# A chunked RWKV-6 recurrence and a star-ReLU layer in one kernel: turning tiles on TensorE instead of the DMA crossbar, and totals of log w through DRAM

## The chip, the cores and the metric

The kernel runs on one core of a Trainium2 chip. The core has TensorE (PE, the matrix unit, which reads SBUF and writes PSUM), VectorE (DVE), ScalarE (ACT) and GpSimd (POOL, which here works on SBUF only), a queue SP that issues DMAs, and 16 DMA engines that move the data. Each engine works through its own instruction list in order; semaphores tie the lists together. The time is the device time of one launch in microseconds. The kernel's time before is 183.34 us, the median of three runs (183.16 to 183.92).

## The reference

Two layers. The first is a recurrence over 768 steps, for 4 batches and 8 heads of width 48; the second is a feed-forward layer on its 3072 x 384 output.

```python
# attention: r, k, v, w are (4, 8, 768, 48), u is (8, 48)
state = zeros((B, H, D, D))
for t in range(S):
    cur = einsum('bhd,bhe->bhde', u[None] * k[t], v[t])
    y[t] = einsum('bhd,bhde->bhe', r[t], state + cur)
    state = w[t][..., None] * state + einsum('bhd,bhe->bhde', k[t], v[t])
# feed-forward: x = y as (3072, 384); w_in (384, 2048); w_out (2048, 384)
h = x @ w_in
g = s * relu(h) ** 2 + b
out = g @ w_out
```

All inputs and the output are float32 in DRAM. w lies between 0.8 and 0.95.

## The kernel before

The sequence is cut into chunks of 128 steps, so there are 6 chunks x 4 batches = 24 chunk-batches, numbered n = 0 to 23 in the order of work. The first four are handled in pairs with a packed layout; from 4 on each goes by itself, chunk by chunk over the four batches, so that n + 4 is the next chunk of the same batch. Two chunk-batches make one token tile T of 256 tokens, 12 tiles in all.

One chunk-batch takes these steps; the words are those of the order (below), the lines those of the kernel before.

- `load n.x` (L297): w, r, k, v by SP, 192 KB each. `ln` (L329, ACT): log w into a bf16 tile whose heads are padded from 48 to 64 columns.
- `cum` (L383, PE): exclusive running sums of log w over the chunk, by a product with a triangular matrix, into PSUM (`cums`). For chunks that are not the last of the sequence, four more products with one column of ones (L416) give the chunk's total of log w per channel, with channels on partitions: columns 384 to 387 of the same PSUM tile. Last chunks (n of 20 and above) need no totals.
- `exp` (L424, ACT): exp of the running sums, and of the totals in the same instruction (388 columns). From n = 6 on, `inc` (L460, DVE) adds log w to the running sum to make it inclusive, and `exn` (L471, ACT) takes exp of its negative.
- `mul` (L477, DVE): r and k times these, into `prd` (bf16, 128 x 1024 with padding).
- `tr` (L533, PE) turns `prd` with eight products against the identity into a PSUM tile `trps`, and `tev` (L556) copies that to the SBUF tile `RK`. For n >= DTK = 9 there is no `tr`; `tev` is then one DMA transpose on SP (`dtrans`, L572), from SBUF to SBUF.
- `mt` (L589, PE): k-by-r products per head, for a pair of chunk-batches. `msk` (L625, DVE) masks them. `ymm` (L640, PE): the chunk's output, from the masked products and from the state that came in. `yev` (L751, DVE) adds the diagonal term `yd`, which POOL and DVE make by `rkp`, `rku`, `cd`, `yd` (L343 to L381).
- `dmm` (L713, PE), `sup` (L765, DVE) and `st` (L791, POOL) make the new state: new = (old + d) * exp(total), where `l2` (L510, POOL) spreads exp of the totals over two column groups. The state is needed by `ymm` and `sup` of n + 4.
- `xtr` (L800, PE) turns the output x (three products) and `xev` (L814) copies it into `xT`, the token tile's operand. For n >= DTX = 18 one DMA transpose (`dxtr`, L581) does both.

Per token tile follow 8 blocks `g1` (L851, PE, six products of 256 columns: x by w_in), each followed by `relu` (L869, ACT) and `sq` (L877, ACT or DVE), and 8 blocks `g2` (L894, PE, four products of 384 columns: g by w_out), `oev` (L909, DVE) and `store` (L922, SP). The feed-forward weights are loaded in five pieces (`li`, `lo`) and cast to bf16 (`ci`, `co`) early on.

The order of all this is written out by hand in a text, ORDER (L41): every word is one step, and the engines get their instructions in that order. `@A`, `@D`, `@P` after a word put the step on ACT, DVE or POOL; `+9` stands for nine warm-up products on PE. A table of rings (L970) holds how many buffers each kind of tile has: `P=6` PSUM buffers serve `cum`, `tr`, `mt`, `xtr`, `ymm`, `dmm` and `g1` alike, `rh=4` buffers stand between relu and square. The planner only verifies that the text respects the dependencies and the rings; its costs set nothing on the chip.

There is also code for taking totals by DMA (`lam`, `lamg`, `by_row`); with LAM = 24 no chunk-batch uses it before the change.

Of the kernel before, what the change touches and what calls it, by code (L numbers as in the profile page):

```python
# [8 lines left out]
FP32 = mybir.dt.float32  # L9
# [16 lines left out]
PKD = 1.55  # L26
ONE = 6
DTK = 9
DTX = 18
DK2 = 24  # L30
DX2 = 24
LAM = 24
# [9 lines left out]
load0.0 load0.2 +9 load0.1 ln0 load2.2 cum0.0 load0.3 cum1.0 exp0.0 +1 u_mm exp0.1 load2.0 exp1.0  # L42
rkp0 mul0.0 load2.1 cum1.1 mul0.1 exp1.1 rkp1 load4.0 u_ev@D tr0 mul1.0 +4 tev0@A mul1.1 rku1 li0
tr1 load2.3 exl0 +2 rku0 cd1 tev1@A li1 ln2 cd0 mt0 load4.1 msk1.0 cum2.0 rkp3 l21 li2 msk0.0 +2 yd1
ln4 exp2.0 cum3.0 cum3.1 msk0.1 l20 rku3 ci0@A load4.2 msk1.1 cum4.0 +3 vb0@D vb1@A yd0 mul2.0
exp2.1 lo0 dmm0 exp3.1 mul2.1 +2 li3 exp3.0 li4 exl2 mul3.0 exp4.0 l23 cum4.1 sup0 vb3@P ymm0.0
exp4.1 tr2 rkp2 ci1@A mul3.1 st0 ymm0.1 sup1 ydm0 vb2@A l24 lo1 rku2 ymi0 yev0@D tr3 yev1@A tev2@D
xtr0 tev3@A xtr1 l22 +1 st1 xev0@D cd2 xev1@A mt2 cd3 rkp4 ci2@A g10.0 msk3.0 yd3 g10.1 msk2.0
relu0.0 lo2 msk2.1 yd2 ymm2.0 relu0.1 g10.2 msk3.1 rku4 dmm2 mul4 relu0.2 ymm2.1 ydm2 co0@A ci3@P
g10.3 sq0.1@A sup2 yev2@A cd4 st2 ymi2 sq0.2@A xtr2 sup3 yev3@A csred0@D lo3 g10.4 sq0.0@A ci4@D  # L50
load5.0 xev2@A xtr3 g10.5 load6.0 relu0.3 co1@D xev3@A lo4 g10.6 csred1@D sq0.3@A load5.1 g11.0
relu0.6 csadd1@D g11.1 relu0.4 co2@D relu0.5 g20.0 csred2@D sq0.4@A g10.7 sq0.6@A g11.2 sq0.5@A
relu0.7 g11.3 csadd2@D relu1.0 load5.2 g20.1 co3@D relu1.3 g20.4 relu1.1 load6.1 csred3@D ln5 g20.5
ln6 tr4 sq0.7@A cum6.0 csadd3@P tev4@D cum5.0 relu1.2 g11.4 inc6 sq1.3@A load6.2 g11.5 sq1.0@A co4@D
cum5.1 exp5.0 g11.6 small2 csred4@D exp5.1 load5.3 exp6.0 g20.6 exn6 g11.7 relu1.6 mul5 relu1.4
small g20.7 sq1.1@A load4.3 csadd4@D g20.2 relu1.7 load7.0 cssplit tr5 sq1.2@A load8.0 relu1.5 mul6
csspread g20.3 csevac load8.1 tev5@D vb5@P tr6 sq1.5@A rkp5 oev0.0 tev6@A mt4 load9.0 oev0.1 g21.4
l25 msk4.0 sq1.4@A rku5 load7.1 dmm5 g21.0 vb4@A msk5.0 g21.5 ln7 load7.2 sup5 rkp6 sq1.7@A msk4.1
cum7.0 st5 yd4 dmm4 load8.2 g21.1 load9.1 ln8 exp7.0 sup4 l26 cum8.0 cd5 st4 ymm4 ln9 msk5.1 yd5
g21.6 sq1.6@A inc7 load6.3 ymm5 exp8.0 st3 yev4 cum9.0 exn7 g21.7 yev5 rku6 inc8 xtr4 xtr5 g21.2  # L60
xev4@A load10.0 mul7 l27 xev5@A g21.3 exn8 load9.2 inc9 rkp7 g12.0 oev1.1 exp9.0 load9.3 g12.1 mul8
relu2.0 l28 relu2.1 load7.3 g12.2 cd6 l29 sq2.1@A sq2.0@D yd6 g12.3 load11.0 tr7 load10.1 exn9
oev1.0 relu2.2 g12.4 tev7@D vb6@P relu2.3 load8.3 g12.5 relu2.4 sq2.3@D mul9 sq2.4@A mt6 relu2.5
g22.4 msk7.0 store0.0 sq2.2@A vb7@P g12.6 msk6.0 sq2.5@A rkp9 load11.1 tev9 msk6.1 dmm6 g22.0
relu2.6 rku7 ln10 sup6 g12.7 load10.2 ln11 msk7.1 tr8 rku9 relu2.7 cd7 g22.1 sq2.7@A cum10.0 cd9
tev8@A load12.1 vb9@A dmm7 ymm6 rkp8 inc10 g22.5 rku8 yev6 load12.0 cum11.0 sup7 g22.6 yd9 xtr6
inc11 exp11.0 exp10.0 g22.2 yd7 xev6@A cd8 load15.0 ymm7 sq2.6@A vb8@P mt8 yev7 exn11 load13.0 st6
g22.3 exn10 msk8.0 st7 store0.1 xtr7 g22.7 xev7@D load11.2 msk8.1 rkp10 dmm9 load10.3 g13.0 store1.1
msk9.0 l210 g13.1 rku10 msk9.1 relu3.0 load11.3 g13.2 sq3.0@A sup9 yd8 mul10 g13.3 relu3.2 load12.2
st9 g13.4 ln12 relu3.1 g13.5 oev2.0 sq3.1@A ymm9 oev2.1 relu3.3 dmm8 g13.6 mul11 rkp11 relu3.4 rku11  # L70
sq3.3@A g13.7 load14.0 load13.1 sq3.2@A g23.0 sup8 relu3.5 g23.4 yev9 relu3.6 sq3.4@D l211 tev11
load13.2 sq3.5@A ymm8 cum12.0 relu3.7 yev8 xtr9 vb11@P g23.1 st8 ln13 inc12 tev10 xtr8 sq3.7@D g23.5
xev8@A exp12.0 g23.6 xev9@D store1.0 exn12 vb10@D load12.3 sq3.6@D cum13.0 ln14 dmm11 mul12 g14.0
exp13.0 ln15 g14.1 inc13 tev12 cd10 g23.2 exn13 cd11 load14.1 relu4.1 yd10 dmm10 g14.2 sup10 rkp13
g23.3 sup11 relu4.2 load14.2 mul13 g14.3 sq4.1@A rkp12 relu4.0 g14.4 oev3.0 relu4.3 tev13 mt10
sq4.0@A rku13 g23.7 relu4.4 load15.1 msk10.0 sq4.3@A g14.5 msk10.1 l213 sq4.2@A l212 rku12 msk11.0
cum14.0 g14.6 relu4.5 msk11.1 load13.3 exp14.0 st10 cum15.0 exp15.0 g14.7 oev3.1 vb12@A ymm11 inc15
load17.0 relu4.7 yd11 ymm10 sq4.4@D sq4.5@A g24.4 store2.0 st11 relu4.6 sq4.7@A g24.0 cd12 load16.0
inc14 load15.2 exn14 sq4.6@A rkp14 g24.5 yd12 cd13 mt12 yev10 load16.1 vb13@A rku14 yev11 g24.1
msk12.0 g24.6 msk12.1 store2.1 xtr10 xtr11 load19.1 msk13.0 g24.2 xev10@A xev11@A msk13.1 dmm12 ln16  # L80
g24.7 exn15 cd14 load16.2 g15.0 rkp15 mul14 g15.1 relu5.0 l215 g15.2 relu5.1 load19.2 sup12 g15.3
sq5.0@A mul15 dmm13 st12 relu5.2 ymm12 g24.3 relu5.3 load14.3 sup13 sq5.3@A oev4.1 g15.4 rku15
sq5.2@A yev12 g15.5 ln17 tev15 sq5.1@D yd13 tev14 relu5.4 ymm13 g15.6 oev4.0 cd15 load15.3 st13
cum17.0 relu5.6 xtr12 g15.7 xev12@D relu5.5 rkp16 yev13 g25.4 sq5.4@A load17.1 inc17 sq5.6@A l214
load18.0 g25.0 cum16.0 rku16 relu5.7 inc16 store3.0 xtr13 vb14@A rkp19 g25.5 xev13@D store3.1
exp17.0 exp16.0 g25.1 load17.2 l217 sq5.5@A rku19 load18.1 g16.0 load17.3 dmm14 yd15 g16.1 relu6.0
sup14 exn16 cd16 yd14 relu6.1 mt14 exn17 g25.6 msk14.0 load19.0 vb15@A g16.2 msk14.1 sq5.7@A
load16.3 mul16 g16.3 rkp17 sq6.0@A relu6.2 g16.4 msk15.0 g25.2 msk15.1 sq6.1@A relu6.3 load18.2
rku17 ln18 g16.5 sq6.3@A mul17 g16.6 tev16 st14 sq6.2@A dmm15 relu6.6 load20.3 cum18.0 ymm14 sup15
relu6.4 g25.7 cd19 l216 tev17 relu6.5 g25.3 vb16@P oev5.1 ln19 st15 g16.7 oev5.0 load20.0 rkp18  # L90
ymm15 exp18.0 vb17@D relu6.7 g26.0 yev14 sq6.4@A load21.0 inc18 rku18 cum19.0 xtr14 yev15 exn18
g26.4 inc19 xev14@A l218 g26.5 store4.1 sq6.5@A load22.0 sq6.7@A xtr15 dmm17 g26.1 load20.1 xev15@D
exp19.0 mul18 sq6.6@A g17.0 load18.3 exn19 sup17 dmm16 g17.1 relu7.0 sup16 cd17 g17.2 relu7.1
sq7.0@D g17.3 mul19 relu7.2 yd17 load19.3 g17.4 ln20 st17 relu7.3 mt16 load21.1 sq7.3@A g26.2
msk17.0 relu7.4 load20.2 ln21 st16 g26.3 msk16.0 sq7.2@A g17.5 msk17.1 yd16 store4.0 sq7.1@A
load21.2 msk16.1 cum21.0 g26.6 vb18@P tev19 oev6.0 ln22 l219 g17.6 vb19@P relu7.5 sq7.4@D inc21
store5.1 yd19 ymm17 relu7.6 tev18 ymm16 cum20.0 g27.4 yev16 rkp20 exp20.0 load23.0 yev17 exp21.0
g27.5 exn21 inc20 rku20 xtr16 sq7.5@D xtr17 g26.7 xev16@A load21.3 exn20 rkp21 dmm19 xev17@D g17.7
cd18 g18.0 sup19 relu7.7 rku21 mul20 store5.0 g18.1 sq7.7@A vb20@P yd18 cum22.0 g27.6 relu8.0 g18.2
oev6.1 tev20 exp22.0 mul21 relu8.1 load22.1 g18.3 sq7.6@A supn20 load22.2 relu8.2 g18.4 relu8.3  # L100
g27.0 inc22 sq8.0@A supn21 dmm18 cd20 mt18 sq8.1@D tev21 sup18 g27.7 relu8.4 msk19.0 sq8.3@A
# [1225 lines left out]
```

## Time and profile before

| | |
|---|---|
| median of three runs | 183.34 us |
| the profiled execution | 183.5 us, span 181.7 us |
| PE busy | 171.8 us, 95% |
| DVE / ACT / POOL busy | 142.8 / 142.2 / 105.0 us |
| DMA transposes | 15 of `prd`, 6 of `x_sb` |
| granted TensorE clock | 1.00 |
| DMA moved | 34.72 MB, mean 191 GB/s |

The span goes from the first instruction to the last; the time of the execution has 1.8 us more around it. Busy time is a union: two instructions that overlap on one engine count once. PE's products are pipelined, and the end of each is modelled, so that a product's own duration (273 ns for 256 columns) is longer than its distance to the next. The chain of waits is followed back from the last instruction; it gives each piece of work the time by which it moved the end.

### The profile page before, as it was taken

Reading aid. Unit: us, or ns where it says so; the run is one execution under the profiler, and the core shown is the slowest. Engines: PE = TensorE matmul, PEld = TensorE weight load, DVE = VectorE, ACT = ScalarE, POOL = GpSimd, SP = SyncE. Lnnn points to the kernel's source line nnn. Section 1 sums busy time; section 2 is a strip of 40 time slices with the busy share of each in tenths; the row PEclk is TensorE's granted clock in tenths of the full one; section 3 lists DMA queues with packets and bytes.
Section 4 is the critical chain, followed back from the end, with each engine's and each line's share of the span. In section 5 each row is a group of like instructions: output and inputs, shape, how many; then the busy total and the mean of one; then the engine's idle time right before and its main releaser. Section 6 shows DMA issues by size and latency. Waiting matters only on the chain.

```text
span 181.7 us, 4868 instructions
## 1 busy us (share of the span) xinstructions
PE 171.8 (95%) x1874; PEld 131.9 (73%) x1876; DVE 142.8 (79%) x257; ACT 142.2 (78%) x279; POOL 105.0 (58%) x139
## 2 busy tenths in 40 slices
PE   7989879998999989999999999999999999999993
PEld 2455669765686769688689688787877696888762
DVE  7679999999999979798998497898998976330222
ACT  3589899998889559979878899898896188479920
POOL 3889860229599699559869759289809560000000
PEclk9999999999999999999999999999999999999999
DMA  5999999999898998999989889999994794220013
GB/s 154 323 324 343 387 350 274 260 184 206 167 207 178 187 187 182 199 171 183 232 186 195 212 172 202 208 199 243 160 206 100 158 238 153 69 60 11 0 43 132
DMA packets 116554, 34.72 MB, mean 191 GB/s; under 512 B 110898, under 2 KB 114739, under 8 KB 116531
## 3 DMA queue, kind: packets, MB, share of 16 engines
q1 hardware_dynamic: 116528, 34.42, 81.6%
q8 instruction: 14, 0.23, 0.5%
q14 instruction: 10, 0.07, 0.1%
q10 hardware_dynamic: 2, 0.00, 0.0%
HBM read 25.17 MB, written 4.72 MB: 164 GB/s over the span
## 4 chain that ended last, share of the span: by engine, by line
PE 64%; DVE 10%; DMA 7%; POOL 6%; issue 5%; ACT 4%; SPq 1%; DVEq 0%; ACTq 0%; POOLq 0%
PE o_ps L901 27%; PE h_ps L858 26%; DMA wo_st<-in_moe_w_out_dram 4%; DMA rkt<-in_k_dram 3%; PE mt_ps L617 2%; POOL rkp L346 2%; PE y_ps L676 2%; DVE prd L489 2%; PE y_ps L667 2%; POOL rku L352 1%; POOL yd L375 1%; PE d_ps L741 1%; ACT rh L871 1%; PE cums L410 1%; PE xt_ps L804 1%
## 5 line engine op out<-in xcount | busy, mean ns | idle before, releaser
L901 PE MATMUL o_ps<-w_out,gT 128*128 128x384 bf16 (+2 forms) x400 | 71.8, 320 | 0.5 <-ACT gT L881 0.5
L858 PE MATMUL h_ps<-xT,w_in 128*128 128x256 bf16 x576 | 70.9, 273 | 1.1 <-POOL w_in L983 0.6
L871 ACT ACTIVATE rh<-h_ps 128x512 bf16<-128x512 f32 x96 | 54.4, 597 | 16.6 <-PE h_ps L858 15.7
L858 PEld LDWEIGHTS <-w_in 128*128 128x128 bf16 x576 | 59.9, 110 | 6.1 <-issue 1.0
L901 PEld LDWEIGHTS <-gT 128*128 128x128 bf16 x400 | 36.1, 98 | 19.7 <-ACT gT L881 0.7
L881 ACT ACTIVATE gT<-rh 128x512 bf16<-128x512 bf16 x78 | 47.4, 634 | 0.5
L352 POOL TENSOR_TENSOR rku<-rkp,u_bc 128x384 f32<-128x384 f32 x24 | 27.7, 1158 | 2.2 <-DVE cd L369 1.6
L346 POOL TENSOR_TENSOR rkp<-rkt 128x384 f32<-128x384 f32 x20 | 21.3, 1068 | 11.2 <-DMA rkt<-in_k_dram 9.4
L629 DVE TENSOR_TENSOR mt_sb<-mt_ps,tri_strict 128x512 bf16<-128x512 f32 x40 | 25.4, 681 | 1.9 <-PE mt_ps L617 1.8
L375 POOL TENSOR_TENSOR yd<-vt,cd 128x384 bf16<-128x384 f32 x20 | 17.6, 884 | 11.0 <-DVE cd L369 10.7
L489 DVE TENSOR_TENSOR prd<-rkt,E 128x768 bf16<-128x768 f32 x20 | 23.7, 1187 | 0.3 <-ACT E L473 0.3
L912 DVE SCALAR_TENSOR_TENSOR o_sb<-o_ps,s_bc,bconst 128x384 f32<-128x384 f32 (+2 forms) x25 | 14.6, 594 | 6.4 <-PE o_ps L901 6.3
L883 DVE TENSOR_TENSOR gT<-rh 128x512 bf16<-128x512 bf16 x18 | 9.6, 536 | 10.2 <-ACT rh L871 10.2
L793 POOL TENSOR_TENSOR st<-stmp,l 128x384 bf16<-128x384 bf16 x16 | 15.5, 972 | 0.8 <-DVE stmp L784 0.8
L758 DVE TENSOR_TENSOR x_sb<-y_ps,yd 128x384 bf16<-128x384 f32 x20 | 10.7, 549 | 5.3 <-PE y_ps L676 5.2
L369 DVE TENSOR_REDUCE cd<-rku 128x8 f32<-128x384 f32 x24 | 12.8, 542 | 1.4 <-POOL rku L352 1.4
L448 ACT ACTIVATE E<-cums 128x388 f32<-128x388 f32 (+1 forms) x22 | 10.4, 496 | 4.3 <-DVE inc L463 2.4
L784 DVE TENSOR_TENSOR stmp<-d_ps,st 128x384 bf16<-128x384 f32 x16 | 8.7, 550 | 3.2 <-PE d_ps L741 3.1
L473 ACT ACTIVATE E<-inc 128x384 f32<-128x384 f32 x18 | 9.3, 525 | 1.5 <-DVE inc L463 1.4
L1286 PE MATMUL warm_ps<-warm_sb 128*128 128x512 bf16 x22 | 7.7, 477 | 1.3 <-DVE warm_sb L1242 1.2
L983 POOL CAST vb<-vt 128x384 bf16<-128x384 f32 x9 | 5.6, 629 | 4.1 <-DMA vt<-in_v_dram 4.1
L676 PE MATMUL y_ps<-vb,mt_sb 128*128 128x48 bf16 x160 | 7.3, 183 | 0.0
(112 smaller groups left out, 200.6 us busy)
## 6 DMA issues: line engine op xcount, KB each, us to landing
wt<-in_w_dram SPq DMA_DIRECT2D x20, 192.0 KB, 3.9
rkt<-in_r_dram SPq DMA_DIRECT2D x20, 192.0 KB, 3.8
rkt<-in_k_dram SPq DMA_DIRECT2D x20, 192.0 KB, 3.7
vt<-in_v_dram SPq DMA_DIRECT2D x20, 192.0 KB, 3.6
out_dram<-o_sb SPq DMA_DIRECT2D x19, 192.0 KB, 3.0
wi_st<-in_moe_w_in_dram SPq DMA_DIRECT2D x3, 768.0 KB, 7.5
wo_st<-in_moe_w_out_dram SPq DMA_DIRECT2D x3, 768.0 KB, 7.0
pkt<-in_w_dram SPq DMA_DIRECT2D x2, 384.0 KB, 4.1
```

Of the source, the lines that this page charges most:

```text
L346: nc.gpsimd.tensor_tensor(out=rkp, in0=c["r"], in1=c["k"], op=ALU.mult)
L352: nc.gpsimd.tensor_tensor(out=rku.rearrange("t h d -> t (h d)"), in0=c["rkp"].rearrange("t h d -> t (h d)"), in1=u_bc, op=ALU.mult,)
L369: nc.vector.reduce_sum(out=cd, in_=c["rku"], axis=AX.X)
L375: nc.gpsimd.tensor_tensor(out=yd, in0=c["v"], in1=c["cd"].unsqueeze(2).to_broadcast([128, H, D]), op=ALU.mult,)
L489: nc.vector.tensor_tensor(out=prd[:, :, :, 0:D], in0=c["rk"], in1=c["E"][:, :, 0:HD].rearrange("t x (h d) -> t x h d", h=H), op=ALU.mult,)
L629: nc.vector.tensor_tensor(out=c["mt"][:, sg], in0=c["mt_ps"][sg], in1=(masks[:, n % 2] if packed(n) else tri_strict) .unsqueeze(1) .to_bro ...
L793: nc.gpsimd.tensor_tensor(out=c["st_new"], in0=c["stmp"].rearrange("q p (g e) -> q p g e", g=2), in1=c["l2"].unsqueeze(3).to_broadcast([12 ...
L858: nc.tensor.matmul(ps[:, f, :], lhsT=w_in_sb[PIECE[ft]][:, kt, :].rearrange("p (m j) -> p j m", j=PIECES[PIECE[ft]])[:, ft - F0[PIECE[ft]] ...
L871: nc.scalar.activation(out=rh, in_=hs[T, i], func=AF.Relu)
L881: nc.scalar.activation(out=g, in_=rh, func=AF.Square)
L901: nc.tensor.matmul(os_[T, k][:, cols], lhsT=gT[T][:, ft, tt * 128 : (tt + 1) * 128], rhs=w_out_sb[PIECE[ft]][:, ft - F0[PIECE[ft]], cols], ...
L912: nc.vector.scalar_tensor_tensor(out=o_sb[:, cols], in0=os_.pop((T, k))[:, cols], scalar=s_bc, in1=bconst[:, cols], op0=ALU.mult, op1=ALU.add,
```

## The change

Six things change together.

1. DTK, DTX, DK2, DX2 go to 99: no chunk-batch uses the DMA crossbar. All 24 are turned by `tr` and `tev`, and all 24 outputs by `xtr` and `xev`.
2. LAM goes to 9: chunk-batches 9 to 19 take their totals of log w by DMA. `lam` writes row 127 of the inclusive sums, 512 padded floats, to a DRAM row; `lamg` reads it back so that channels lie on partitions, four floats each; `exl` on ACT takes the exp, and `l2` stays on POOL. The four one-column products of these eleven are gone.
3. The inclusive sums go to two fixed tiles with heads padded to 64 columns (`incs`), the padding cleared once, so that one DMA reads the row back instead of two.
4. `sq` may go to POOL; 16 of 96 do.
5. The warm-up operand shares its memory with `cs_sum`, and the clearing of `lams` goes.
6. ORDER is a new text: 1160 words instead of 1105. The engines of many `tev`, `xev`, `vb`, `co` and `sq` change with it, and the loads' order too.

```diff
-DTK = 9
-DTX = 18
-DK2 = 24
-DX2 = 24
-LAM = 24
+DTK = 99
+DTX = 99
+DK2 = 99
+DX2 = 99
+LAM = 9
...
+    incs = [const.tile([128, H, 64], FP32, name=f"inc{i}", tag=f"inc{i}") for i in range(2)]
...
         if x == 0:
             E = work.tile([128, 2, HD + 16], FP32, name="E", tag="E", bufs=2)
-            c["E"], c["lam"] = E, E[:, 0, HD : HD + HP]
+            c["E"] = E
             if cc < NCH - 1 and not by_row(n):
+                c["lam"] = E[:, 0, HD : HD + HP]
                 w = HD + HP
...
     def expl(n):
         c = cb[n]
+        if not packed(n):
+            t = work.tile([128, 16], FP32, name="lamr", tag="lamr", bufs=NLT)
+            c["lam"] = t[:, 0:HP]
+            nc.scalar.activation(out=c["lam"], in_=lams[:, n % NLT, 0:HP], func=AF.Exp)
+            return
...
     def incl(n):
         c = cb[n]
-        t = work.tile([128, HD], FP32, name="inc", tag="inc", bufs=2)
+        t = incs[incl_no[0] % 2]
+        if incl_no[0] < 2:
+            nc.vector.memset(t[:, :, D:64], 0.0)
+        incl_no[0] += 1
+        c["inc_row"] = t.rearrange("t h d -> t (h d)")[127:128]
+        c["inc"] = t[:, :, 0:D]
...
     def lamrow(n):
         c = cb[n]
-        c["tot"] = dram.tile([1, HD], FP32, name="tot", tag="tot")
-        nc.sync.dma_start(out=c["tot"], in_=c["inc"][127:128])
+        c["tot"] = dram.tile([1, H * 64], FP32, name="tot", tag="tot")
+        nc.sync.dma_start(out=c["tot"], in_=c["inc_row"])
 
     def lamget(n):
-        row = cb[n]["tot"].rearrange("o (p g d) -> g d (o p)", g=2, p=HP)
-        t = lams[:, n % NLT, 0 : 2 * HP].rearrange("q (p g) -> q g p", g=2)
-        for g in range(2):
-            nc.sync.dma_start(out=t[64 * g : 64 * g + D, g], in_=row[g])
+        nc.sync.dma_start(
+            out=lams[:, n % NLT, 0:HP],
+            in_=cb[n]["tot"].rearrange("o (p q) -> q (o p)", q=128),
+        )
...
         if pl.ops["sq", T, i]["eng"] == "ACT":
             nc.scalar.activation(out=g, in_=rh, func=AF.Square)
         else:
-            nc.vector.tensor_tensor(out=g, in0=rh, in1=rh, op=ALU.mult)
+            eng = nc.gpsimd if pl.ops["sq", T, i]["eng"] == "POOL" else nc.vector
+            eng.tensor_tensor(out=g, in0=rh, in1=rh, op=ALU.mult)
...
-    warm_sb = const.tile([128, 2 * TOK], BF16, name="warm_sb", tag="warm_sb")
+    warm_sb = cs_sum.rearrange("p x n -> p (x n)")[:, 0 : 2 * TOK]
...
-    nc.gpsimd.memset(lams, -10000.0)
```

Two stretches of the new text, the second from the end, show how the words stand (`tr` and `tev` of batches 9 and 8, then the squares of the last tile on POOL):

```
tr8 exp10.0 yev7 g22.1 yev6 rku9 relu2.7 sq2.7@A load11.3 vb8@A cum11.0 tr9 tev8@D sq2.6@A st7
load15.0 xtr6 st6 tev9@A xtr7 store0.0 g22.6 exn10 vb9@D exp11.0 xev6@D g22.2 rkp10 inc11 load13.0
xev7@D g22.7 cd8 g13.0 cd9 lamg9 exn11 mul10 relu3.0 g13.1 store0.1 g13.2 mul11 relu3.1 load10.3
...
sq10.7@D g29.2 g210.5 xev23@D sq10.4@A g29.3 g111.0 oev9.0 g111.1 relu11.0 g111.2 sq10.6@P sq11.0@P
store9.0 relu11.1 g111.3 relu11.2 sq11.1@A g210.0 g210.6 sq11.2@D g111.4 g111.5 relu11.4 g111.6
sq11.4@P relu11.5 g210.7 relu11.3 g111.7 oev10.1 sq11.3@D relu11.7 store10.1 g210.1 sq11.7@P g210.2
g210.3 g211.0 oev10.0 g211.1 sq11.5@A relu11.6 sq11.6@P g211.4 g211.2 g211.5 store10.0 g211.3 g211.6
```

## The prediction

> **What bounds the kernel now.** I read the page's busy shares and slices first, then busy time by stretch, then the chain that ended last, then the costliest groups, and the DMA issues last.
>
> ```profile
> PE 171.8 (95%) x1874; PEld 131.9 (73%) x1876; DVE 142.8 (79%) x257; ACT 142.2 (78%) x279; POOL 105.0 (58%) x139
> ...
> PEclk9999999999999999999999999999999999999999
> DMA  5999999999898998999989889999994794220013
> ```
>
> TensorE (PE) is busy 95% of the span at its full granted clock. The 16 DMA engines are nearly as full, which would make them a suspect; the stretches decide. Their columns are length, then busy time and count of PE, of its weight loads, of VectorE (DVE), ScalarE (ACT) and GpSimd (POOL), then clock, DMA share and GB/s.
>
> ```profile
> 1.20:60.00 58.80, 54.01 (x630) 38.39 (x633) 54.21 (x99) 50.41 (x97) 38.90 (x58) 1.00 1.00 262
> 60.00:160.00 100.00, 99.17 (x1096) 78.99 (x1095) 83.44 (x148) 79.82 (x161) 65.54 (x76) 1.00 0.87 182
> 160.00:181.70 21.70, 18.58 (x152) 14.49 (x150) 4.82 (x10) 12.01 (x23) 0.00 (x0) 1.00 0.15 51
> ```
>
> From 60 to 160 us PE stands still for 0.8 us of 100, although DMA is at 0.87. Before 60 it stands still for 4.8 us, with DVE at 54.21 of 58.80. After 160 it stops only for the last store, 3.1 us. The chain (start, length, what) says whether "busy" is really full:
>
> ```profile
> 59.46 0.45 PE trps L538 x8
> ...
> 67.36 3.93 PE h_ps L858 x36
> ...
> 73.14 1.30 PE o_ps L901 x8
> ...
> 75.05 0.19 PE xt_ps L804 x3
> ...
> 75.89 0.17 PE xt_ps L804 x3
> ...
> 77.52 0.08 PE cums L416 x4
> ```
>
> 36 products of 256 columns in 3.93 us are 109 ns each and 8 of 384 columns in 1.30 us are 162 ns each, back to back, block after block: nothing to squeeze. So behind the first 60 us every microsecond of PE work that is added is a microsecond of time, and one removed is one saved.
>
> ```profile
> L881 ACT ACTIVATE gT<-rh 128x512 bf16<-128x512 bf16 x78 | 47.4, 634 | 0.5
> ...
> L793 POOL TENSOR_TENSOR st<-stmp,l 128x384 bf16<-128x384 bf16 x16 | 15.5, 972 | 0.8 <-DVE stmp L784 0.8
> ...
> L554 DVE COPY RK<-trps 128x1024 bf16<-128x1024 bf16 x4 | 2.7, 684 | 0.4 <-PE trps L538 0.2
> ...
> L554 DVE COPY xT<-xt_ps 128x384 bf16<-128x384 bf16 x7 | 2.5, 352 | 2.3 <-PE xt_ps L804 2.3
> ```
>
> These price the evacuations (mean ns behind the comma).
>
> ```profile
> RK<-prd SPq DMA_TRANSPOSE x15, 3.7
> xT<-x_sb SPq DMA_TRANSPOSE x6, 2.6
> ...
> b_bc<-in_moe_b_dram SPq DMA_DIRECT2D x1, 0.5 KB, 3.0
> ```
>
> The 21 crossbar turns land 3.7 and 2.6 us after their issue; the first is issued at 58.0 us, so all lie in the stretch in which PE is full.
>
> **The change, part by part.** *Turns.* 15 chunk-batches (9 to 23) get `trans`: 8 products, 0.45 us by the chain. 15 x 0.45 = +6.75. Six (18 to 23) get `xtr`: 3 products, 0.17 to 0.19, +1.1. All of it lies where PE has no idle time, on the path.
>
> A page of the Trainium skill speaks against this part more than my row does: "TensorE: Matmul & The Clock Gate", section "Back-to-back issue gap", gives about 81 ns for each product of 128 columns in a real stream. The row gives 0.45/8 = 56 ns. By the page the 15 x 8 + 6 x 3 = 138 added products would be an estimated 11.2 us, and the whole sum an estimated 194.4. The same page (Part 4) says that transposes do not count as PE work for the clock; this trace has 126 of them with the clock at 1.00 throughout. The row decides.
>
> *One-column products.* `cum` of batches 9 to 19 loses its four products: 0.08 us by the chain, 11 x 0.08 = -0.9. Warm-up products go from 24 to 23: -0.2, in the head.
>
> PE sum: 6.75 + 1.1 - 0.9 - 0.2 = **+6.7**.
>
> *Evacuations and who pays.* By the two word lists, DVE copies 17 RK tiles instead of 4 (+13 x 0.684 = 8.9), 15 xT instead of 7 (+2.8) and casts three more vb (+1.6), and loses three w_out casts (-2.5): +11 in all. ACT loses 15 squares (-9.5) and gains 11 exps of four columns, RK copies and casts: about -3. POOL gains 16 squares of 128x512 and loses five casts. No row has such a square on POOL: from below a cast of half its operands, 629 ns for 384 columns, so 0.84; from above `rku` in f32, 1158 ns for 384, so 1.54. I take 1.3, scaled from L793 (972), the nearest: bf16 with bf16. POOL comes to about 105 + 16 x 1.3 - 3 = 123 of 190, still the emptiest. These engines are beside the path as long as PE does not wait for them. In 60 to 160, where some 11 us of the DVE work land, DVE goes from 83.4 in 100 to about 95 in 107: 89%. The cover is thin, so I bound what PE waits for. From below 0: in 80 to 100 us before, DVE is at 18.11 of 20 and PE at 20.00. From above 8: in 40 to 60 DVE is at 19.61 of 20 and PE idle 1.51, times 107/20. A second look at the same cost: before, PE waited 1.3 + 0.7 + 0.4 us at the nine batches that it turned itself, 0.27 each, times 15 = 4.0, mostly in the head with nothing else to do. Since 89% lies by the first row, I take **+1.0**.
>
> *PSUM.* Each added turn holds one of the six P buffers from PE to the copy's end; that is in the same bound, because a late copy is what makes it dear.
>
> *Totals by DMA.* Per batch: `lam` (one row to DRAM) waits for `inc` in SP's queue, `lamg` waits there for that row to land, `exl` on ACT waits for `lamg`, `l2` on POOL for `exl`, then `st`. Behind `lamg` on SP stand loads and stores; behind `exl` on ACT stand relu and square, whose lateness PE would feel. Landing: 1.5 from below (the 48 KB store), 7.5 from above (the slowest of the issues); I take 3.0, the 0.5 KB issue. Adding PE's row times over the new word list, `lam` to `lamg` has 2.8 to 14 us of PE work between and `lamg` to `exl` 5.8 to 18: at 3.0 all hidden, on SP a few tenths are waited. At 7.5 five of the eleven `exl` would stand up to 1.7 us, some 6 us of ACT, of which ACT's own 20 idle us in 60 to 160 take a part: 0 to 4 on PE. Taken: 0.
>
> *DMA freed.* The crossbar's share goes and the loads have room. By the view of waits POOL waited 9.4 us for k loads, but PE stood still 0.8 us in the stretch concerned, so there is nothing to win there. Taken: 0; from below -0.8.
>
> *Order in the head.* Up to the first h_ps block of the third token tile (50.9 us before) both lists hold 41 us of PE work, while DVE's pieces sum to 48.2 against 47.0 us. DVE being at 92% there, the head cannot shrink by much: -2 to +2, taken 0. At the end four of the last tile's eight squares are on POOL; PE has 8 blocks (some 4.9 us) between the last h_ps and the block that needs the last of them, against two squares in a row, 2.6: hidden, up to +1 at 1.54 each.
>
> Sum on the profiled execution (183.5: span 181.7 and 1.8 around it): 183.5 + 6.7 + 1.0 = 191.2. The median of the three runs is 0.16 lower: **191.0 us**.
>
> **Rivals.** *DVE becomes the bound* (193.5 to 199). For it: +11 us on an engine at 83%, and four of the eight pairs (12, 14, 18, 22) leave 0.7 to 1.6 us of PE work between the place of the last RK copy in the word list and the `mt` that needs it, where the crossbar's turns had 5.6 to 8.6. Against it: PE has h_ps and o_ps blocks to fill with. Price +8 at the upper row: 183.3 + 6.7 + 8 = 198.
>
> *The totals are late* (192 to 197): landing near 7.5, ACT stands, 191 + 4 = 195. Against it: the row of 3.0.
>
> *The order fills PE's gaps* (184.3 to 188.5): half of the 4.8 us of the head and the 0.8 behind it go: 183.3 + 6.7 - 2.8 = 187.2. For it: the order is rewritten whole. Against it: DVE at 92% in the head.
>
> *Not slower* (below 184.3; 0.5%, or 0.9 us, is about what a measurement of this kernel can tell from no change). One mechanism: the head. With every idle us of PE gone between 1.2 and 160 us, 5.6, the time is 183.3 + 6.7 - 5.6 = 184.4; it takes this and shorter turns to get under. It decides if the third tile's first h_ps block starts before about 45 us. Against it: DVE's 48 us of pieces ahead of that block.
>
> That the change does not do what it says I rule out: the new queues hold 24 `trans`, 24 `xtr` and no crossbar turn.
>
> **How the numbers follow.** Forecast (188.5 to 193.5) 0.60; DVE bound 0.20; totals late 0.05; gaps filled 0.12; not slower 0.03, split evenly about no change and faster. The range leaves out about one in ten on each side: 187.3 to 196.5. Nearly all of it has one sign.
>
> **What would show it.** In the changed profile: L538's counterpart x192 and xt_ps x72 instead of 72 and 54; PE at 0.45 per turn; PE busy 99% from 60 to about 167 us, with PE's total about 178; DVE near 154 and POOL near 123; the DMA row falling below 9 in the middle with no gain. Wrong would be: PE idle over 3 us between 60 and 165 with DVE copies as releaser (too low a forecast), ACT waiting for `lams`, or the third tile's h_ps well ahead of 50.9 us (too high).

## The result and the profile after

The changed kernel takes 191.54 us (median of three runs, 190.74 to 192.15) against 183.34 before: a ratio of 1.0436, 95% interval 1.0365 to 1.0508. It is 8.2 us slower. Its profiled execution is 192.15 us with a span of 190.4, 8.7 above the span before, and the accounts below are made between those two spans. (This execution is the slowest of its three.) Executions that lie over 1.5% above the fastest of their kernel are left out of the ratios; there are two of them in each of three kernels below: the one with doubled copies of `RK`, the one with more output turns by crossbar, and the old order with totals by DMA.

From the page of the changed kernel, the busy times, the clock, the DMA row and the queue of the loads, stores and turns:

```profile
PE 180.1 (95%) x1969; PEld 138.6 (73%) x1969; DVE 152.9 (80%) x280; ACT 139.5 (73%) x278; POOL 115.6 (61%) x150
...
PEclk9999999999999999999999999999999999999999
DMA  6999999999898869989889899672021011011022
...
q1 hardware_dynamic: 104022, 29.94, 66.3%
```

The queue of the kernel before:

```profile
q1 hardware_dynamic: 116528, 34.42, 81.6%
```

PE is still the engine that is busy 95% of the span, at the full clock. The DMA row falls off at about 120 us; before, it was nearly full up to 136 us and between 0.4 and 0.9 from there to 154. On queue q1 the packets took 66.3% of 190.4 us, 126.2, where before they took 81.6% of 181.7, 148.3: 22 us less of all 16 engines, and the kernel is slower. Now the same stretches as before (length, busy time and count of PE, its weight loads, DVE, ACT, POOL, then clock, DMA share and GB/s):

```profile
1.20:60.00 58.80, 53.64 (x611) 37.20 (x612) 52.29 (x103) 46.71 (x88) 38.12 (x59) 1.00 1.01 263
60.00:165.00 105.00, 103.77 (x1160) 83.74 (x1158) 92.30 (x160) 83.14 (x174) 71.73 (x82) 1.00 0.61 130
165.00:190.40 25.40, 22.64 (x203) 17.61 (x200) 8.04 (x17) 9.62 (x17) 5.17 (x5) 1.00 0.13 47
```

And the same 105 us of the kernel before:

```profile
60.00:165.00 105.00, 104.17 (x1133) 82.88 (x1132) 84.39 (x150) 83.74 (x169) 65.54 (x76) 1.00 0.84 176
```

In the 105 us from 60 on PE stands still for 1.23; in the kernel before it was 0.83. DVE is busy 92.30 of 105, 88%, and PE hardly waits for it. DMA at 0.61 instead of 0.84 buys nothing there. The groups that the prediction had to price without a row, or by a far one (mean ns behind the comma):

```profile
L895 POOL TENSOR_TENSOR gT<-rh 128x512 bf16<-128x512 bf16 x16 | 18.1, 1136 | 43.4 <-ACT rh L882 43.4
...
L549 PE MATMUL trps<-shift,prd 128*128 128x128 bf16 x192 | 14.9, 219 | 2.1 <-DVE prd L506 1.0
...
L565 DVE COPY RK<-trps 128x1024 bf16<-128x1024 bf16 x17 | 11.5, 680 | 0.6 <-PE trps L549 0.5
```

All 192 products of the 24 turns are there. A product's own 219 ns overlap the next product's; what a turn adds to the path is read from the chain (start, length, what):

```profile
87.84 0.45 PE trps L549 x8
...
117.62 0.33 PE xt_ps L815 x6
...
134.18 0.89 PE trps L549 x16
```

Eight products cost 0.45 us and sixteen 0.89, six of the output's 0.33: the prices that the rows before had given. The totals that now go by DMA:

```profile
L522 SPq DMA_DIRECT2D lams<-tot x11: 365/681/1175, 65.2 to 123.3; - x11
...
DMA to landing us min/median/max: 2.3/2.7/3.0
```

They land 2.3 to 3.0 us after their issue. ACT is not seen waiting for them. Last, PE's timeline at the place where the head ends (start, length, what): the first h_ps block (a word `g1`) of the third token tile, first in the kernel before, then in the changed one.

```profile
50.88 2.78 PE L858 MATMUL h_ps<-xT,w_in 128*128 128x256 bf16 x24
```

```profile
52.87 0.61 PE L549 MATMUL trps<-shift,prd 128*128 128x128 bf16 x8
53.33 1.49 PE L869 MATMUL h_ps<-xT,w_in 128*128 128x256 bf16 x12
```

With that block as a mark, the 8.7 us of span fall into three parts. In front of it: +2.45. From it to PE's last product: 127.7 us before, 134.3 after, +6.6. Behind the last product: 3.1 before, 2.7 after, -0.4. The first part is the least certain: where this block begins varies by a microsecond between kernels with the same words ahead of it (more on this at the head, below).

### The profile page after: what moved, and what is told of

Its sections match the earlier page's. It is cut to its first block, busy times and chain, and to the rows that moved or that the text cites. A ratio compares the mean times of both kernels' runs of the same rounds, so it can differ in the third digit from the quotient of the medians.

```text
span 190.4 us, 5104 instructions
## 1 busy us (share of the span) xinstructions
PE 180.1 (95%) x1969; PEld 138.6 (73%) x1969; DVE 152.9 (80%) x280; ACT 139.5 (73%) x278; POOL 115.6 (61%) x150
## 3 DMA queue, kind: packets, MB, share of 16 engines
q1 hardware_dynamic: 104022, 29.94, 66.3%
## 4 chain that ended last, share of the span: by engine, by line
PE 61%; DVE 14%; ACT 8%; DMA 8%; issue 4%; SPq 1%; POOL 1%; DVEq 0%; ACTq 0%
PE o_ps L913 24%; PE h_ps L869 21%; DMA wo_st<-in_moe_w_out_dram 5%; PE trps L549 3%; PE warm_ps L1299 3%; DVE prd L506 3%; DVE wo_st L954 2%; PE mt_ps L628 2%; DMA rkt<-in_r_dram 2%; ACT rh L882 2%; DVE prd L499 2%; DMA rkt<-in_k_dram 2%; ACT gT L892 2%; PE y_ps L687 1%; PE xt_ps L815 1%
## 5 line engine op out<-in xcount | busy, mean ns | idle before, releaser
L869 PE MATMUL h_ps<-xT,w_in 128*128 128x256 bf16 x576 | 72.3, 273 | 1.2 <-ACT xT L563 0.5
L913 PE MATMUL o_ps<-w_out,gT 128*128 128x384 bf16 (+2 forms) x400 | 73.3, 320 | 0.1
L895 POOL TENSOR_TENSOR gT<-rh 128x512 bf16<-128x512 bf16 x16 | 18.1, 1136 | 43.4 <-ACT rh L882 43.4
L892 ACT ACTIVATE gT<-rh 128x512 bf16<-128x512 bf16 x63 | 38.3, 633 | 0.3
L356 POOL TENSOR_TENSOR rku<-rkp,u_bc 128x384 f32<-128x384 f32 x24 | 26.0, 1089 | 2.5 <-DVE cd L373 1.4
L549 PE MATMUL trps<-shift,prd 128*128 128x128 bf16 x192 | 14.9, 219 | 2.1 <-DVE prd L506 1.0
L549 PEld LDWEIGHTS <-prd 128*128 128x128 bf16 x192 | 11.9, 98 | 5.4 <-DVE prd L506 2.6
L453 ACT ACTIVATE E<-cums 128x384 f32<-128x384 f32 (+1 forms) x22 | 10.8, 493 | 5.0 <-DVE inc L480 2.8
L769 DVE TENSOR_TENSOR x_sb<-y_ps,yd 128x384 bf16<-128x384 f32 x20 | 10.6, 548 | 4.3 <-PE y_ps L687 4.2
L895 DVE TENSOR_TENSOR gT<-rh 128x512 bf16<-128x512 bf16 x17 | 8.4, 501 | 6.0 <-ACT rh L882 6.0
L565 DVE COPY RK<-trps 128x1024 bf16<-128x1024 bf16 x17 | 11.5, 680 | 0.6 <-PE trps L549 0.5
```

Of the source, the lines that this page charges most:

```text
L356: nc.gpsimd.tensor_tensor(out=rku.rearrange("t h d -> t (h d)"), in0=c["rkp"].rearrange("t h d -> t (h d)"), in1=u_bc, op=ALU.mult,)
L549: nc.tensor.matmul(ps[:, x * HP + p, :], lhsT=c["prd"][:, x, 2 * p : 2 * p + 2, :].rearrange("t h d -> t (h d)"), rhs=identity, is_transpo ...
L869: nc.tensor.matmul(ps[:, f, :], lhsT=w_in_sb[PIECE[ft]][:, kt, :].rearrange("p (m j) -> p j m", j=PIECES[PIECE[ft]])[:, ft - F0[PIECE[ft]] ...
L892: nc.scalar.activation(out=g, in_=rh, func=AF.Square)
L895: eng.tensor_tensor(out=g, in0=rh, in1=rh, op=ALU.mult)
L913: nc.tensor.matmul(os_[T, k][:, cols], lhsT=gT[T][:, ft, tt * 128 : (tt + 1) * 128], rhs=w_out_sb[PIECE[ft]][:, ft - F0[PIECE[ft]], cols], ...
```

## The experiments

The theory that they test is the prediction's: the time is the added PE work of the turns, laid on an engine without idle time. Its rivals are VectorE as the new bound, the totals, and the new order (its head, or as a whole).

**All turns on PE, in the old order.** The words `tr n` and `tev n` take the crossbar's places in the text before or stand up to some five microseconds behind them, `xtr` and `xev` likewise; nothing else is changed, no totals by DMA, no square on POOL. (All in the very same places is not possible with six PSUM buffers: `xtr12`, for one, would then need a buffer that only `relu5.5` frees, which stands behind it.)

```diff
-DTK = 9
-DTX = 18
+DTK = 99
+DTX = 99
...
-rkp9 load11.1 tev9 msk6.1 dmm6
+rkp9 load11.1 tr9 msk6.1 dmm6
...
-rku7 ln10 sup6 g12.7 load10.2
+rku7 ln10 sup6 g12.7 tev9@A load10.2
```

> The kernel before in its own order, with only the crossbar turns replaced: chunk-batches 9 to 23 are turned by eight products and a copy put where the DMA transposes stood or up to some five microseconds later, outputs 18 to 23 by three products and a copy; totals of log w still by one-column products, no square on GpSimd. Theory (TensorE's work is the time): 183.3 + 15 x 0.45 + 6 x 0.18 = 191.2 us, with up to 1.5 more for words that nobody tuned: 190.5 to 193. Rival one (the new order, not the turns, makes the kernel slower): under 187. Rival two (the copies fill VectorE, TensorE waits for them): over 194, with TensorE idle over 3 us between 60 and 165 us and copies as the releaser.

192.07 us, ratio 1.0473 (1.0433 to 1.0514) to the kernel before, measured beside it at 183.14: +8.9, where the products alone are 15 x 0.45 + 1.1 = 7.85. By the profiles 0.5 of it lie ahead of the third tile's first block (51.41 us against 50.88), where no word was changed; from there to the last product it takes 135.8 us against 127.7, +8.1. Its windows:

```profile
60.00:165.00 105.00, 104.36 (x1200) 84.32 (x1199) 90.57 (x161) 81.97 (x163) 64.57 (x77) 1.00 0.58 129
```

PE's idle time is 0.64 of 105, no more than before. The turns alone, without the new order, the POOL squares or the totals, cost what the whole change costs. The new order is therefore not what makes the changed kernel slow, and as a whole it doesn't make it measurably faster either: the two ratios' intervals overlap.

**The same PE work without any turn.** Old kernel, crossbar kept; two products of 512 columns into an unused buffer beside each of the 15 crossbar turns.

```diff
-rkp9 load11.1 tev9 msk6.1 dmm6
+rkp9 load11.1 tev9 +2 msk6.1 dmm6
```

> The kernel before with its crossbar turns, plus two products of 512 columns without use near each of the 15 crossbar turns of chunk-batches 9 to 23: 30 x 0.215 = 6.4 us of TensorE work and nothing else (no copy, no DMA less; each pair takes one turn of a PSUM buffer). Theory (TensorE has no idle time there): 183.3 + 6.4 = 189.7 us, within 1. Rival (TensorE's busy time hides gaps that added work can fill): under 188.

189.88 us, ratio 1.0349 (1.0305 to 1.0393): +6.7 by the medians, 5.6 to 7.2 by the interval, for 6.4 us of useless products.

```profile
60.00:165.00 105.00, 104.39 (x1119) 81.64 (x1124) 82.80 (x146) 79.95 (x160) 66.22 (x78) 1.00 0.83 175
```

Here DVE is no busier than before (82.80 of 105 against 84.39) and DMA is as full as before (0.83), yet a microsecond of PE work is about a microsecond of time. That is the mechanism by itself: no copy, no DMA and no order is needed for it. It is not exact: in the profiled execution, the fastest of four, the third tile's first block begins at 51.49 us and the last product ends 132.8 us later, 5.1 more than before, so that some of the added work went into gaps. Set beside the run above, in the same order, it also says that the 0.83 against 0.58 of DMA share between them is worth nothing that shows.

**VectorE: late, or merely busy?** Two kernels add useless work to VectorE in the changed kernel. The first makes the copy of `RK` twice for the 15 batches from 9 on (15 x 0.68 = 10.2 us), so that each turn's reader, and the release of its PSUM buffer, come at least 0.68 us later (for four of the 15 the first copy is on ACT, and VectorE's has to wait for it):

```diff
         move(("tev", n), RK, c["trps"])
+        if n >= 9:
+            nc.vector.tensor_copy(out=RK, in_=c["trps"])
```

> The changed kernel with the RK tile of chunk-batches 9 to 23 copied a second time on VectorE: 15 x 0.68 = 10.2 us more for VectorE and no other work. It measures how thick the cover is. VectorE stands at 92.3 of 105 between 60 and 165 us; with 10 more it would be at 97%. Theory (TensorE is the bound, VectorE is close behind): 192.5 to 196. If VectorE's time had room to spare: under 192. If VectorE already were the bound: 191.5 + 10 = 201.

Ratio 1.0921 (1.0856 to 1.0986), which is 200.0 us at 183.14 for the kernel before beside it: some 8.9 us above the changed kernel's ratio. That is 4 us over the range expected if TensorE is the bound, and near the 201 of VectorE as the bound. The clock does not explain it: one execution kept 1.00 throughout and took 199.89. So the next kernel has to tell VectorE's load from the delay. The second puts about as much work on VectorE (14 scale-adds of 0.6, some 8.4 us) where it is off the path, on the way to the store:

```diff
-        nc.vector.scalar_tensor_tensor(
-            out=o_sb[:, cols],
...
+        for _ in range(2 if 2 <= T <= 8 else 1):
+            nc.vector.scalar_tensor_tensor(
+                out=o_sb[:, cols],
```

> The changed kernel with the output's scale-and-add done twice on VectorE for token tiles 2 to 8: 14 x 0.61 = 8.5 us more for VectorE, at a place that TensorE does not soon wait for. With double RK copies (10.2 us, just ahead of the product that reads them) the time grew by 10.4. If VectorE's occupancy is as much the bound as TensorE's: + 7 to 9, 198.5 to 200.5. If it was the delay between turn and reader that counted there: + 1 to 4, 192.5 to 195.5.

192.79 us, ratio 1.0506 (1.0468 to 1.0544): 1.25 above the changed kernel by the medians, 1.5 by the profiles from the third tile's first block to the last product (135.8 us against 134.3).

```profile
60.00:165.00 105.00, 102.84 (x1137) 82.41 (x1136) 96.80 (x172) 81.80 (x172) 70.61 (x82) 1.00 0.59 126
```

VectorE is busy 96.80 of 105 here, 92%, and PE's idle time rises only from 1.23 to 2.16. So VectorE's load is not the bound of the changed kernel; but copies added between a turn and its reader were paid for nearly in full, 0.87 of each added microsecond. Whether PE pays for the late `RK` or for the late PSUM buffer was not told apart.

**The head.** The changed kernel with the old text's words, engines and warm-up up to the third tile's first block, spliced to the new text from there.

```diff
-load0.0 load0.1 +9 load0.2 ln0 load2.0 load0.3 load2.1 cum1.0 cum0.0 load2.2 u_mm exp0.0 exp0.1 rkp0
+load0.0 load0.2 +9 load0.1 ln0 load2.2 cum0.0 load0.3 cum1.0 exp0.0 +1 u_mm exp0.1 load2.0 exp1.0 rkp0
...
 g12.6 dmm7
```

> The changed kernel with the head of its order replaced: up to the first block of the third token tile the words of the kernel before, then the seven words that this leaves out, then the new order. TensorE's and all other work stays the same. In the changed kernel that block starts at 53.3 us instead of 50.9, with 0.45 us more TensorE work ahead of it (one turn). Theory (the late head is time lost for good, since TensorE is full behind it): 191.5 - 2.0 = 189.5 us, 188.8 to 190.3. Rival (the lateness is caught up behind, or VectorE sets the pace there): 191 or more.

190.54 us, ratio 1.0389 (1.0361 to 1.0417). On its PE timeline:

```profile
51.62 1.47 PE L866 MATMUL h_ps<-xT,w_in 128*128 128x256 bf16 x12
```

The block starts 1.7 us earlier than in the changed kernel, its span is 1.6 us shorter (188.8), and its median 1.0 lower, 0.2 above the expected range and 0.5 below the rival's; its ratio lies inside the interval of the changed kernel's own. The new head is the later one by the traces, and going back to the old one gains some of it, half of what was expected by the medians. It is the fastest kernel with all turns on PE, and still 3.9% behind the kernel before. It also says what the rest of the change is worth: against the old order with all turns on PE (1.0473, 1.0433 to 1.0514) the intervals do not overlap, and with the old head on both sides the new words behind it, the totals by DMA and the squares on POOL together gain some 1.5 us, 0.9 of which the missing one-column products would account for.

**The totals, taken out of the new order and put into the old one.** First the changed kernel with one-column products, then the old order and its crossbar turns with totals by DMA (this kernel has the changed kernel's padded sums and its shared warm-up operand).

```diff
-LAM = 9
+LAM = 24
...
-cum10.0 relu2.6 lam9 rkp9 sup7
+cum10.0 relu2.6 rkp9 sup7
...
-cd8 g13.0 cd9 lamg9 exn11 mul10
+cd8 g13.0 cd9 exn11 mul10
```

> The changed kernel with the totals of chunk-batches 9 to 19 by one-column products again and no small DMAs; the spreading of the totals moves forward to where its input's buffer is needed. Theory (TensorE's work is the time): 191.5 + 11 x 0.08 = 192.4 us, at 0.11 each 192.8. Rival (the two DMAs and the waits for them on SP and ScalarE cost as much as they save): 191.5 or less.

191.95 us, ratio 1.0478 (1.0438 to 1.0518): 0.4 above the changed kernel by the medians. By the profiles it takes 0.6 more from the third tile's first block to the last product (134.9 against 134.3). That can be told neither from nothing nor from the 0.9 of the products.

```diff
-LAM = 24
+LAM = 9
...
-load9.3 g12.1 mul8 relu2.0
+load9.3 g12.1 lam9 mul8 relu2.0
...
-relu2.5 g22.4 msk7.0 store0.0
+relu2.5 g22.4 lamg9 msk7.0 store0.0
```

> The kernel before in its own order and with its crossbar turns, with only the totals of chunk-batches 9 to 19 by the two small DMAs. Theory (TensorE's work is the time): 183.3 - 0.9 = 182.4 us. Rival (the DMA engines, 0.87 busy between 60 and 160 us, have no room, or the 512 pieces of four bytes are dear): 183.3 or more, with longer landings of the loads.

Ratio 1.0071 (1.0042 to 1.01), which is 184.7 us at 183.41 for the kernel before beside it: 1.3 us slower, though 0.9 us of products is gone. Its windows and its queue:

```profile
60.00:160.00 100.00, 98.38 (x1054) 77.53 (x1052) 83.78 (x149) 79.66 (x171) 65.68 (x78) 1.00 0.93 183
```

```profile
q1 hardware_dynamic: 122358, 34.46, 84.2%
```

DMA goes from 0.87 to 0.93 of that stretch and PE's idle time from 0.83 to 1.62. The 22 small DMAs took 84.2% of 182.7 less 81.6% of 181.7, about 5.6 us of all 16 engines, half a microsecond for each pair, although they carry 4 KB a pair. They are not the cause of all of the 1.3: in the profile, 1.0 us longer than that of the kernel before, 0.4 lies ahead of the third tile's first block (51.27 us against 50.88), before any total goes by DMA. What is left says that beside the crossbar the small DMAs save nothing and cost about the 0.9 that they should have gained; whether by their DMA time, by SP's queue or by the eleven exps on ACT was not told apart. Without the crossbar, in the changed kernel, they cost nothing that shows.

**The crossbar put back into the new order.** If the turns' 6.75 us are the whole loss, the new order with `RK` by crossbar should be about as fast as the kernel before. Three kernels: the DMA transpose right behind `mul` with the totals by DMA, the same with one-column totals, and the latter with each transpose placed some 4 us of PE work later.

```diff
-DTK = 99
-DK2 = 99
+DTK = 9
+DK2 = 24
...
-load11.2 tr8 exp10.0 yev7
+load11.2 tr8 tev9 exp10.0 yev7
...
-cum11.0 tr9 tev8@D sq2.6@A
+cum11.0 tev8@D sq2.6@A
```

> The changed kernel in its own order, with the 15 turns of chunk-batches 9 to 23 given back to the DMA crossbar, issued as soon after the multiplication as the ring of four RK tiles lets them; outputs 18 to 23 still by TensorE, totals still by DMA. Theory (TensorE's work is the time): 191.5 - 15 x 0.45 = 184.8 us, up to 1.5 more where a crossbar turn lands late: 184.3 to 186.5. Rival (the new order itself costs the time): 189 or more. VectorE's busy time falls by some 8 us in both.

198.89 us, ratio 1.0857 (1.0805 to 1.091). The expectation was missed by 14 us; the time lies in the rival's range, that of the new order as the cost (189 or more), which the runs above speak against.

```profile
60.00:160.00 100.00, 89.43 (x905) 68.23 (x904) 77.11 (x133) 72.52 (x156) 70.61 (x80) 0.98 0.89 171
```

```profile
q1 hardware_dynamic: 119862, 33.87, 77.1%
```

PE stands still 10.6 of 100 us. Against the changed kernel the queue's packets took 77.1% of 196.0 less 126.2, 24.9 us more for 15 turns: 1.66 us of all 16 engines for each. The one-column variant (the words `lam`, `lamg` and `exl` go as well):

```diff
-LAM = 9
+LAM = 24
```

> The changed kernel in its own order with the 15 turns of chunk-batches 9 to 23 by the DMA crossbar, as before, but now with one-column products for the totals, so without the 22 small DMAs and their waits in SP's queue. If those overfilled the DMA engines and the queue: 192.0 - 6.75 = 185.2 us, 184.5 to 187.5. If the crossbar's own DMA time (15 x 1.7 us of all 16 engines, from the two DMA shares) is what the new order has no room for: 193 or more, with loads of v and k landing late and VectorE or ScalarE waiting for them.

195.88 us, ratio 1.0678 (1.0625 to 1.0732). Without the small DMAs it is 3 us better, and still slow, in the range of the crossbar's own DMA time (193 or more). What SP's queue waited for, the time, how often and the longest:

```profile
SPq L580 <- DVE prd L500: 13.0, 6, 5.1
```

In the kernel before the like line is much shorter:

```profile
SPq L575 <- DVE prd L489: 2.4, 3, 1.6
```

So in this order the transpose's word stands where SP reaches it long before `prd` is made, and the loads behind it in SP's list wait too. The third kernel tests that:

```diff
-load11.2 tr8 tev9 exp10.0 yev7 g22.1 yev6
+load11.2 tr8 exp10.0 yev7 g22.1 tev9 yev6
...
-store0.1 g13.2 mul11 tev11 tev10 relu3.1
+store0.1 g13.2 mul11 relu3.1
...
-load14.1 sup8 g13.7 rkp11
+load14.1 sup8 g13.7 tev11 tev10 rkp11
```

> As the run with the crossbar and one-column totals in the new order, but each of the 15 crossbar turns stands in SP's queue later: mostly about four microseconds of TensorE work behind its multiplication instead of directly behind it, and 4.6 or more ahead of the product that reads it. Theory (there SP stood 13 us in turns that waited for the multiplication, with loads queued behind them; the crossbar itself has room): the waits of SP for prd fall below 4 us and the time to 185 to 188. Rival (the crossbar's 1.7 us of all DMA engines per turn is what the new order's loads have no room for): 193 or more, DMA share near 1.0 from 60 to 140 us.

196.27 us, ratio 1.0711 (1.0671 to 1.0751): no better. Its waits of SP, and its windows:

```profile
SPq L580 <- DVE prd L500: 12.3, 4, 5.4
SPq L580 <- PE h_ps L863: 11.3, 7, 2.9
```

```profile
60.00:140.00 80.00, 71.73 (x759) 55.39 (x757) 64.42 (x114) 58.49 (x122) 59.33 (x68) 0.98 0.94 189
```

The waits for `prd` did not go away with the move, and at the same transposes SP waited another 11.3 us behind PE's products, so the run doesn't test what it was made for. DMA is at 0.94 here while PE loses 8.3 of 80 us. But the share alone says little, for in the kernel before it is as high, and PE loses 0.8:

```profile
60.00:140.00 80.00, 79.17 (x884) 63.30 (x883) 69.79 (x124) 67.43 (x139) 59.01 (x71) 1.00 0.95 191
```

Two causes stay open: the blocked queue, and too little room in DMA for what was held up to be made good later. What is shown is that the crossbar did not go back into this order by those two placements. This is no sign against the price of the turns, which the first two experiments measure directly.

**More of the crossbar in the old order.** The opposite of the change: 8 more outputs (batches 10 to 17) turned by DMA, 24 products less on PE.

```diff
-DTX = 18
+DTX = 10
...
-msk12.0 g24.6 msk12.1 store2.1 xtr10 xtr11 load19.1
+msk12.0 g24.6 msk12.1 store2.1 load19.1
...
-cd13 mt12 yev10 load16.1
+cd13 mt12 yev10 xev10 load16.1
```

> The kernel before with eight more output turns by the crossbar (chunk-batches 10 to 17), each issued right behind the addition that makes the tile: 8 x 0.18 = 1.4 us of TensorE work less, and no copies on ScalarE and VectorE. Theory (TensorE's work is the time): 183.2 - 1.4 = 181.8 us, the one candidate for a kernel faster than both. Rival (DMA engines and SP's queue are full, the turns land too late for the block that reads them 2 to 3 us later): 184 or more.

Ratio 1.059 (1.0498 to 1.0682), 194.4 us at 183.61 for the kernel before beside it: +10.8 instead of -1.4. What PE waited for, and the windows:

```profile
PE h_ps L854 <- DMA xT<-x_sb: 8.9, 4, 2.7
```

```profile
60.00:140.00 80.00, 70.45 (x757) 54.94 (x755) 62.08 (x106) 59.12 (x120) 54.99 (x66) 0.98 0.94 186
```

PE waits for four of the turned outputs, 8.9 us in all. A turn by crossbar lands 2.4 us after its issue (median, 2.3 to 4.0), and DMA is at 0.94 of these 80 us, no more than the 0.95 of the kernel before. So also in the old order, the one that suits the crossbar, eight more turns on it, placed as here, cost far more than the PE work that they save; taking turns off it is not the only way to lose. Whether the DMA engines or SP's queue made them late was not told apart.

## Why the prediction was right, point by point

The total was 0.5 us low (191.0 against 191.54). Its cause is the one that the runs show, the turns' products on a full engine. Two terms of the sum were off and nearly cancelled, so that the centre was met in part by luck.

*Turns and PE sum, +6.7: right.* The products cost 0.45 a turn in the chain after as before. The two kernels in the stretch from the third tile's first block to the last product, the kernel before first:

```profile
50.88:178.60 127.72, 126.43 (x1340) 100.98 (x1337) 96.68 (x169) 99.89 (x198) 74.09 (x87) 1.00 0.77 162
```

```profile
53.33:187.66 134.33, 133.08 (x1431) 107.07 (x1428) 105.93 (x186) 99.39 (x204) 83.57 (x96) 1.00 0.55 118
```

Behind the third tile's first block lie the 15 added turns, while that of batch 7 has moved in front of it, so that 6.75 - 0.45 + 1.1 - 0.9 = 6.5 was to be expected there; 6.6 was measured. On TensorE's price the prediction weighed 56 ns for a product of 128 columns by the row against some 81 by the Trainium skill ("TensorE: Matmul & The Clock Gate", section "Back-to-back issue gap"), which would have made it 194.4. The chain after gives 0.89/16 = 56 ns, and the time agrees with the row.

*Waits behind VectorE's copies, 0 to 8, taken +1.0: too high.* From the block to the last product PE stood still 1.25 us after and 1.29 before. VectorE's load came out as worked out (152.9 us; 88% of the stretch), but load is not delay: 8.4 us more of it off the path cost 1.25 (192.79), while 10.2 between turns and their readers cost about 8.9 (200.0). The estimate scaled PE's idle time by VectorE's load, and that was the weak place of it.

*Head, -2 to +2, taken 0: too low.* In the two profiles the block began 2.45 us later, 0.45 of it the turn that the new order has moved in front. The other 2.0 is the upper bound itself. The same profiles ahead of the block, the kernel before first:

```profile
1.20:50.88 49.68, 45.32 (x536) 30.89 (x539) 45.47 (x87) 42.36 (x81) 30.35 (x49) 1.00 1.01 275
```

```profile
1.20:53.33 52.13, 46.97 (x542) 31.49 (x542) 46.38 (x93) 40.07 (x75) 31.45 (x50) 1.00 1.01 270
```

PE's idle time accounts for 0.8 of the 2.0 (5.16 us against 4.36). The other 1.2 is PE time that counts as busy, and half of that is seen at the very start. The kernel before, then the changed one:

```profile
5.16 0.48 PE L392 MATMUL cums<-logw_two,hs_pos 128*128 128x384 bf16 x2
```

```profile
5.52 1.15 PE L396 MATMUL cums<-logw_two,hs_pos 128*128 128x384 bf16 x3
```

Before, products of 384 columns start 0.16 us apart here; after, some 0.3 us, as if at half the pace, although the granted clock reads 1.00 in both. Four of them cost 0.6 us more. This is not the new words' doing, for in two other kernels with the same words the three products take 0.65 us, here in the one with doubled scale-adds:

```profile
5.40 0.65 PE L396 MATMUL cums<-logw_two,hs_pos 128*128 128x384 bf16 x3
```

PE's total, 180.1 instead of the 178 foreseen, has this 1.2 in it too.

How late the new head is by its own words is seen better over all kernels that share one. The block begins between 52.14 and 53.33 us in the six that have the new one and a clock of 1.00 up to there, on average at 52.69 (a seventh, with doubled copies, had a granted clock of 0.57 from 43 to 47 us and has 54.75), and between 50.69 and 51.49 us in the five that have the old one, on average at 51.15. One of each group (doubled scale-adds, useless products):

```profile
52.14 1.49 PE L869 MATMUL h_ps<-xT,w_in 128*128 128x256 bf16 x12
```

```profile
51.49 2.78 PE L855 MATMUL h_ps<-xT,w_in 128*128 128x256 bf16 x24
```

That is 1.5 us, 1.1 without the moved turn, and the changed kernel's profile is the latest of its group. With the old head the kernel is 1.0 us faster by the medians. The sums of PE and VectorE work ahead of the block, by which the step took 0, do not show this microsecond; what in the new head delays it was not followed further.

*Totals by DMA, 0: right in the new order.* 2.7 us to landing against the 3.0 taken, ACT not late, POOL's `l` late by 3.5 us in three cases (behind ACT's exp), and no delay on PE that shows. In the old order the same edit ends 1.3 us slower, which the prediction had no reason to ask.

*DMA freed, 0 to -0.8, taken 0: right.* 22 us of all engines' time were given back and nothing came of it.

*Squares on POOL, 1.3 each by the nearest row: 1.136.* POOL came to 115.6 instead of 123; the squares are 2.6 us of the difference, the rest is mostly `l`, 3.2 instead of 6.1, and `rku`, 26.0 instead of 27.7. Neither reaches the path. The end of the kernel is 0.4 shorter, not longer.

*The rivals.* VectorE as the bound fell by its price: PE's idle time behind the head did not rise. The totals were not late. The gaps of the head were not filled, they grew. The kernel that is not slower would have needed the third tile's block at 45 us; it came at 53.33.

## What to carry to other kernels

Where the stretches show an engine without idle time, and its chain shows block after block at a steady pitch, work added to it can be priced by its pitch in that chain, and this price held here to within a tenth by the medians; relief of a resource that is merely busy, here 22 us of DMA time, is worth nothing until it is what PE waits for. A transposition that takes 0.45 us of such an engine was cheaper on a crossbar that takes about 1.6 us of DMA as the old order has it, and dearer in the three kernels here that put it into the new one: order and DMA load have to be tried together. Ask of an added evacuation not how full its engine gets but how long its reader waits.

## What the runs showed of the hardware that was not expected

A pause of TensorE cost more than its length. In the kernel with crossbar and one-column totals in the new order, PE's timeline and the stretches about it show:

```profile
84.56 3.54 PE L863 MATMUL h_ps<-xT,w_in 128*128 128x256 bf16 x18 [2.71 <-ACT xT L557]
```

```profile
82.00:84.00 2.00, 0.00 (x0) 0.10 (x1) 2.00 (x5) 0.35 (x1) 2.00 (x3) 1.00 1.02 199
84.00:86.00 2.00, 1.44 (x7) 0.99 (x7) 1.92 (x3) 0.93 (x3) 2.00 (x3) 0.52 1.06 211
86.00:88.00 2.00, 2.00 (x12) 1.36 (x10) 0.80 (x2) 1.20 (x2) 2.00 (x3) 0.63 0.86 210
88.00:90.00 2.00, 2.00 (x30) 1.85 (x30) 1.53 (x3) 1.80 (x4) 2.00 (x3) 1.00 1.31 105
```

Its columns are those of the windows above. After 2.71 us without a product the granted clock (third column from the end) is 0.52 and then 0.63, and 18 products take 3.54 us instead of 2.14 for the first 18 of the changed kernel's timeline: 1.4 us on top of the pause. The Trainium skill ("TensorE: Matmul & The Clock Gate", section "Why this matters for your kernels") puts the pause from which this happens at about 3 us; here 2.71 was enough.

In these runs the length of one pause does not decide it. In the kernel with the transposes placed later 2.40 us was enough, in the one with more outputs by crossbar 2.50 was not:

```profile
81.30 2.93 PE L863 MATMUL h_ps<-xT,w_in 128*128 128x256 bf16 x13 [2.40 <-ACT xT L557]
```

```profile
82.00:84.00 2.00, 2.00 (x11) 1.36 (x10) 0.79 (x1) 0.60 (x1) 0.75 (x1) 0.50 1.07 214
```

```profile
137.35 1.47 PE L854 MATMUL h_ps<-xT,w_in 128*128 128x256 bf16 x12 [2.50 <-DMA xT<-x_sb]
```

```profile
138.00:142.00 4.00, 4.00 (x35) 3.42 (x33) 1.73 (x4) 3.54 (x7) 0.00 (x0) 1.00 1.23 180
```

And in the kernel with doubled copies of `RK` the clock fell with no pause over 1.21 us near it, behind three microseconds with products in half of them:

```profile
40.00:43.00 3.00, 1.52 (x9) 0.58 (x6) 2.86 (x6) 3.00 (x7) 0.00 (x0) 1.00 0.88 161
43.00:47.00 4.00, 3.45 (x31) 2.76 (x32) 3.98 (x5) 2.25 (x5) 3.55 (x6) 0.57 1.02 203
```

The profiles before and after keep 1.00 throughout, so this plays no part in the result, only in the size of the misses with the crossbar.

Two small ones: a turn of 128x1024 bf16 by the crossbar takes about 1.6 us of all 16 DMA engines (1.66 by the pair of runs above, 1.58 by the pair with one-column totals, 75.2% of 194.2 us less 64.1% of 190.8 over 15), and a pair of totals DMAs of 4 KB in all about 0.35 us in the new order ((126.2 - 64.1% of 190.8)/11) and 0.5 in the old one, far more than their bytes.
